# Seven products for one more block, and written-out lists of steps, in a linear attention and MLP kernel

## The chip, the core and the metric

The kernel runs on one core of a Trainium2 chip. A core has five engines that run side by side, each with a queue of its own that is worked off in order: TensorE (PE, matrix products, with its weight loads PEld), VectorE (DVE), ScalarE (ACT), GpSimd (POOL) and SyncE (SP). On POOL and SP stand mostly the issues of DMA transfers. Engines wait for each other by semaphores. The metric is the device time of one execution in microseconds (us), and the lower the better.

## The reference

Eight batches of 1024 tokens go through attention with 8 heads of 64, whose keys and values are first projected from 1024 positions to 64, and then through an MLP of 512 to 2048 to 512 without a gate.

```python
k_proj = einsum('ks,bhsd->bhkd', E, k)          # 64 x 64 per head
v_proj = einsum('ks,bhsd->bhkd', F, v)
attn = softmax(q @ k_proj.T / 8)                # 1024 x 64 per head
x = (attn @ v_proj) as [8192, 512]              # heads side by side
h = x @ w_in                                    # [8192, 2048]
out = (h * sigmoid(1.702 * h)) @ w_out          # [8192, 512]
```

Inputs and output are float32; the kernel multiplies in bfloat16 and adds up in float32.

## The kernel before

The 8192 tokens are cut into 16 blocks of 512 tokens, two blocks for a batch (block 2 and 3 belong to batch 1, block 4 and 5 to batch 2, and so on). All weights stay in SBUF. For a block the kernel computes scores and exponentials (`expT`), the sums of the exponentials, the values, and from them `xT` (the MLP's input, transposed, 512 rows by 512 tokens); then the first layer with its gelu into `gT`, and the second layer into `o0_sb` and `o1_sb`, which are stored. The work of neighbouring blocks is interleaved, so that the attention of later blocks runs beside the MLP of earlier ones.

**Products.** A plain first layer is `ffn1` (L420): 16 tiles of 4 matmuls of 128 x 128 weights on 512 columns, 64 in all. The other form splits both factors in two by two parts and forms the result with seven products of half size in place of eight (Strassen's scheme in Winograd's form). For the first layer these are the steps `u0` to `u3` (L657): four tiles, each with products P1 to P7 of 4 matmuls on 256 columns. They need sums of parts of `w_in` (`late`, 4 x 2048 elements in each partition, made once), sums of parts of the block's `xT` (`xw`, steps `xs.0` to `xs.3`), and per tile a chain on VectorE and ScalarE: c1 copies the accumulator A into a second bank B, c2 and c3 copy B and G to SBUF, d1 and d2 add, and g11, g12, g21, g22 are the gelus. For the second layer there are the products F1 to F7 (8 matmuls of 256 columns per half), the sums `gs1` to `gs4` of `gT`, the sums `tw` of `w_out`, and copies and additions Fc, Fo and Fd. Blocks 1 to 15 have the second layer in this form, blocks 3 to 15 the first layer.

**What sets the order.** Everything is written in the order in which it is issued; there is no scheduler, and each engine runs its own instructions in that order. Block 0 and 1, and block 2 up to its first layer, are loops over tiles, with further work put behind certain tiles by a table of slots (`at(j, slot, ...)`, L774): behind tile 15 and 16 of block 0, for example, the transposes of q (`q_tr`, L247) for block 1. In the first layer of block 2 stand `w_in_sums` (L477): six operations of VectorE on 2048 elements per partition, with `q_even`, a buffer of q, as temporary. From block 2's second layer on the order is a list of step names, `STEPS` (L586), gone through once for every j from 2 to 15: `u2.P5` is tile 2's product 5 of block j, `va.0+1` the values of block j+1, `F3.0-1` the second layer of block j-1. `AHEAD` (L872) inserts steps at the start, and `due` (L765) leaves out what the loops have done already. `BANK` (L597) gives each kind of tile one of the eight PSUM banks. In the last block the steps of the second layer are replaced by `ffn2_parts` (L517) with a list of its own.

**Other steps named below.** `sc` scores (16 matmuls in 2 halves, L698), `ex` exponentials on ScalarE, `gt` ScalarE's load of the gelu table, `su` and `den` sums of exponentials and their copy, `ga`, `rc`, `sr`, `sb` the gather of those sums into another layout, the reciprocal, the write to DRAM and the broadcast into `rbc`, `va` and `mv` the values and their product with `rbc`, `pj` the projection of k and v of a batch, `kb`, `vq` its copies out of PSUM and `kd` the transposing DMA of k, `qd` that of q, `ld` and `lq` the loads of k, v and q of the next batch on POOL's queue, `hold` a copy of one element on POOL that makes that queue wait for `kd`, `st` the stores. Blocks 1 and 2 take their values in the form `tok`, `x_tr` (L393, L408): values with tokens on the partitions, a reciprocal and product on VectorE, and transposes on PE.

Of the kernel before, what the change touches and what calls it, by code (L numbers as in the profile page):

```python
# [9 lines left out]
F32 = mybir.dt.float32  # L10
# [7 lines left out]
def kernel(ctx, tc, q, k, v, E, F,  # L18
# [53 lines left out]
    def load(b):  # L72
        for what in ("kvq", "kqv", "kvq", "qkv")[min(b, 4) - 1]:
            if what == "q":
                load_q(b)
            elif what == "k":
                load_kv(k, kt, b, "k_sb")
            else:
                load_kv(v, vt, b, "v_sb")
# [95 lines left out]
    kvps, qT, expT, xT, rbc, rdens = {}, {}, {}, {}, {}, {}  # L175
# [127 lines left out]
    def sums(h):  # L303


        def go():
            d_ps = [x_any([P, TB]), bank(5, [P, TB])]
            for p in range(HP):
                for e in range(2):
                    r = HI if (p + e) % 2 else LO  # L310
                    nc.tensor.matmul(d_ps[e][32 * p:32 * p + 32], ones[r, :32], expT[h][r, p, :], start=True, stop=True)
            den = att.tile([P, 2, TB], F32, name="den", bufs=1)
            for e in range(2):
                nc.vector.tensor_copy(den[:, e, :], d_ps[e])
            rdens[h] = den
        return go

    def gather(h):
        def go():
            n = 2 * HP * TB // P  # L320
            rc = att.tile([P, n], F32, name="rc")
            nc.sync.dma_start(out=rc, in_=rdens.pop(h)[0:P:32].rearrange("p e (r n) -> p (e r) n", n=n))
            rdens[h] = rc
        return go

    def spread(h, q=nc.sync, recip=True):
        def go():
            rc = rdens.pop(h)
            n = rc.shape[1]
            if recip:  # L330
                nc.vector.reciprocal(rc, rc)
            rdr = dram.tile([HP, 2, TB], F32, name="rdr")
            q.dma_start(out=rdr.rearrange("p e (r n) -> (p e r) n", n=n), in_=rc)
            rbc[h] = att.tile([P, HP, TB], F32, name="rbc", bufs=1)
            for e, r in enumerate((LO, HI)):
                q.dma_start(out=rbc[h][r], in_=rdr[None, :, e, :].to_broadcast([D, HP, TB]))
        return go

    def norm(h, u):
        def go():  # L340
            e = [expT[h][:, 2 * u + i, :] for i in range(2)]
            d_ps = [x_any([P, TB]) for _ in range(2)]
            eight(d_ps, [ones, ones], e)
            n_ps = [x_any([P, TB]) for _ in range(2)]
            eight(n_ps, [vqs[h // NB2 % 2][:, 2 * u + i, :] for i in range(2)], e)
            for i in range(2):
                rd = att.tile([P, TB], F32, name="rdn")
                nc.vector.reciprocal(rd, d_ps[i])
                nc.vector.tensor_tensor(x_of(h)[:, 2 * u + i, :], n_ps[i], rd, op=ALU.mult)
        return go  # L350

    def values(h, u):
        def go():
            n_ps = [x_any([P, TB]) for _ in range(2)]
            eight(n_ps, [vqs[h // NB2 % 2][:, 2 * u + i, :] for i in range(2)],
                  [expT[h][:, 2 * u + i, :] for i in range(2)])
            for i in range(2):
                nc.vector.tensor_tensor(x_of(h)[:, 2 * u + i, :], n_ps[i], rbc[h][:, 2 * u + i, :], op=ALU.mult)
        return go

# [114 lines left out]
    def w_in_sums():  # L477

        tmp = []

        def tt(out_, in0, in1, op=ALU.subtract):
            def go():
                if not tmp and None in (out_, in0, in1):
                    tmp.append(ldpool.tile([P, KC // 2, DH], F32, name="q_even"))
                a, b, c = (tmp[0] if x is None else x for x in (out_, in0, in1))
                nc.vector.tensor_tensor(a, b, c, op=op)
            return go

        return [tt(late[:, 0], a21, a22, ALU.add), tt(late[:, 2], a11, a21), tt(None, a21, a22, ALU.add),
                tt(None, None, a11), tt(late[:, 3], a12, None), lambda: nc.vector.tensor_copy(late[:, 1], tmp[0])]  # L490
# [26 lines left out]
    def ffn2_parts(j, d, e, f, last):  # L517

        b, c = divmod(j, NB2)
        ov = out[b * S:(b + 1) * S, :].rearrange("(p j) m -> p j m", j=J)[:, c * JB:(c + 1) * JB]
        o = [None, None]
        ops, of = ffn2_ops(j), OF
        gb, u = {}, {}
        split = last is not None

        def mm(i, tc_, first, final):
            a, w = ops[i]
            one = split and of[i] == 2  # L530
            for k in range(FH):
                dst = gb[2 + tc_][:, 0] if one else gb[of[i]][:, tc_]
                nc.tensor.matmul(dst, a[:, k, tc_ * P:(tc_ + 1) * P], w[:, k],  # L533
                                 start=(first and (one or tc_ == 0) and k == 0), stop=(final and k == FH - 1),
                                 skip_group_check=True)

        def tile_of(n, k):
            gb[n] = bank(k, [P, 2, MH])

        def put(t, n=0, m=2, ms=slice(0, DM)):  # L540
            nc.sync.dma_start(out=ov[:, 2 * t + n:2 * t + m, ms], in_=o[t][:, n:m, ms])

        def p(i, tc_):
            def go():
                if (i, tc_) == (1, 0):
                    tile_of(0, d)
                    for t in range(2):
                        o[t] = work.tile([P, 2, DM], F32, name=f"o{t}_sb", bufs=1)
                if (i, tc_) == (5, 0):
                    tile_of(2, f)  # L550
                    u[2] = work.tile([P, 2, MH], F32, name="u2_sb", bufs=1)
                if (i, tc_) == (5, 1) and split:
                    tile_of(3, last)
                mm(i, tc_, i in (1, 5), i in (2, 3, 4) and tc_ == 1)
                if split and i == 5:
                    nc.scalar.copy(u[2][:, tc_], gb[2 + tc_][:, 0])
                elif split and i == 3:
                    nc.vector.tensor_tensor(o[0][:, tc_, MH:], gb[2 + tc_][:, 0], u[1][:, tc_], op=ALU.add)
                    put(0, tc_, tc_ + 1, slice(MH, DM))
                elif tc_ == 0:  # L560
                    pass
                elif i == 1:
                    tile_of(1, e)
                    nc.scalar.copy(gb[1], gb[0])
                elif i == 5:
                    nc.scalar.copy(u[2], gb[2])
                elif i == 6:
                    u[1] = work.tile([P, 2, MH], F32, name="u1_sb", bufs=1)
                    nc.scalar.copy(u[1], gb[1])
                elif i == 2:  # L570
                    nc.scalar.copy(o[0][:, :, :MH], gb[0])
                    if split:
                        put(0, ms=slice(0, MH))
                elif i == 7:
                    nc.vector.tensor_tensor(o[1][:, :, MH:], gb[1], u[2], op=ALU.add)
                elif i == 4:
                    nc.scalar.copy(o[1][:, :, :MH], gb[1])
                    put(1)
                elif i == 3:
                    nc.vector.tensor_tensor(o[0][:, :, MH:], gb[2], u[1], op=ALU.add)  # L580
                    put(0)
            return go

        return {(i, t): p(i, t) for i in range(1, 8) for t in range(2)}

    STEPS = """  # L586
        F3.0-1 u2.c1 Fo1-1 u0.d2 rc+2 F3.1-1 u2.P5 u3.c3 u3.P7 u0.g22 Fd2-1 u2.P6 u0.g12 u2.c2 u2.c3 u2.P2
        u2.g11 u3.P3 va.0+1 u3.d1 st0-1 gs1.0 u3.P2 u3.d2 u3.g11 u2.P3 u3.g12 mv.0.1+1 u2.P7 va.1+1 pj+4 ld+4
        u3.g22 u3.P4 u2.d2 st1-1 u2.g12 u3.g21 u2.d1 mv.0.0+1 kb+4 F1.0 mv.1.0+1 u2.g22 vq.0+4 u2.P4 mv.1.1+1
        gs1.1 u2.g21 vq.1+4 F1.1 u0.P1+1 sr+2 sc.0+3 gs2.0 gs2.1 sc.1+3 Fc1 ex.0.0+3 gs3.0 u1.P1+1 xs.0+1  # L590
        ex.1.1+3 xs.2+1 gs3.1 F2.0 F2.1 ex.1.0+3 xs.1+1 kd+4 ex.0.1+3 F6.0 F6.1 Fc2 u0.c1+1 su+3 u1.c1+1 gt+1
        u0.P6+1 den.0+3 u0.P2+1 Fo0 den.1+3 gs4.1 u1.P6+1 F7.0 u1.P2+1 u1.P5+1 u0.c2+1 F5.0 u1.c2+1 u0.g11+1
        u1.c3+1 F5.1 ga+3 Fc3 u1.P7+1 F7.1 u1.g11+1 xs.3+1 gs4.0 u1.P3+1 u2.P1+1 u0.P5+1 u1.d1+1 u3.P1+1 Fd1
        u0.c3+1 u1.P4+1 F4.0 u0.P7+1 sb+2 u1.d2+1 u0.d1+1 qd+4 lq+4 u1.g21+1 u3.c1+1 F4.1 u1.g12+1 u3.P6+1
        u3.c2+1 u0.P4+1 u1.g22+1 u3.P5+1 u0.P3+1 u0.g21+1
    """.split()
    BANK = dict(FD=0, FB=4, FG=0, A0=6, A1=1, B0=7, B1=3, G0=2, G1=5, S10=5, S11=7, V00=4, V01=0,  # L597
                S00=3, S01=2, V10=6, V11=5, D0=2, D1=5, PJ=1)
    ON_ACT = ('Fc1', 'Fc3', 'c2.2', 'c3.0', 'c3.1', 'c3.2', 'c3.3', 'vq')

# [335 lines left out]
```

## Time and profile before

| what | value |
| --- | --- |
| median of 3 runs | 477.85 us (477.5 to 478.31) |
| profiled execution | 476.44 us |
| its span, first to last instruction | 474.7 us |
| busy PE, PEld, DVE, ACT, POOL | 463.9, 356.2, 316.6, 322.1, 83.2 us |
| DMA | 69.19 MB, mean 146 GB/s |
| granted TensorE clock | 1.00 of full speed throughout |
| a block in the steady part | 54.75 us for two (139.24 to 193.99) |

The profile is one execution, taken by the hardware profiler. Busy time is the time in which an engine had at least one instruction running; the ends of matmuls are modelled, so short gaps of PE can hide in it. Rows of a timeline give start, length, engine, line, operation, the tile written and the tile read, their shapes and count, and in brackets the idle time of the engine before it, with what ended it. The chain of work that ended last is followed back from the last instruction.

### The profile page before, as it was taken

The page shows a single profiled execution, that of the slowest core. Times are in us where ns is not written, and L with a number is a line of the kernel's source. Part 1 is how long each engine was busy: PE and PEld are TensorE (multiplying, and loading weights), DVE is VectorE, ACT ScalarE, POOL GpSimd, SP SyncE. Part 2 cuts the span into 40 slices and gives each one's busy share as a digit, 9 for nine tenths or more (in the row PEclk, how much of TensorE's full clock was granted, in tenths as well). Part 3 has the DMA queues.
Part 4 walks back from the last instruction along what each step waited for, and adds up shares of the span by engine and source line. Part 5 has one row for each costly group of instructions (what it writes and reads, how often), then busy time and mean ns, then how long its engine had stood idle before and what let it go on. Part 6 is the DMA issues. An engine that isn't in the chain of part 4 may idle for free.

```text
span 474.7 us, 10486 instructions
## 1 busy us (share of the span) xinstructions
PE 463.9 (98%) x4323; PEld 356.2 (75%) x4331; DVE 316.6 (67%) x587; ACT 322.1 (68%) x559; POOL 83.2 (18%) x104
## 2 busy tenths in 40 slices
PE   8999999998999999999999999999999999999997
PEld 4644447556778788887878788787888878888885
DVE  4503895498486776858686685868667685958562
ACT  2665456566696777868686786957687786758472
POOL 7562161061051200501050010500000000000000
PEclk9999999999999999999999999999999999999999
DMA  9999999989799999937999299942371403602022
GB/s 169 200 188 207 228 192 152 232 169 180 114 212 207 200 200 238 110 92 162 211 216 130 94 152 214 172 95 97 90 182 38 121 25 91 177 5 90 0 90 90
DMA packets 132964, 69.19 MB, mean 146 GB/s; under 512 B 98341, under 2 KB 122421, under 8 KB 132917
## 3 DMA queue, kind: packets, MB, share of 16 engines
q0 software_dynamic: 86816, 30.43, 57.5%
q1 hardware_dynamic: 46020, 37.84, 32.8%
q8 instruction: 34, 0.56, 0.5%
q10 hardware_dynamic: 80, 0.26, 0.2%
q14 instruction: 14, 0.11, 0.1%
HBM read 72.88 MB, written 16.99 MB: 189 GB/s over the span
## 4 chain that ended last, share of the span: by engine, by line
PE 91%; DMA 3%; ACT 3%; DVE 2%; POOL 1%; issue 1%; DVEq 0%; ACTq 0%; POOLq 0%
PE k_ps L677 34%; PE k_ps L637 33%; PE k_ps L426 9%; PE k_ps L533 5%; PE k_ps L273 3%; PE k_ps L438 3%; PE k_ps L183 3%; DMA v_sb<-in_v_dram 3%; ACT gT L693 1%; PE k_ps L719 1%; DVE xT L713 1%; POOL k_sb L58 0%; POOL v_sb L58 0%; PE k_ps L398 0%; PE k_ps L413 0%
## 5 line engine op out<-in xcount | busy, mean ns | idle before, releaser
L623 DVE TENSOR_TENSOR q_even<-k_ps,q_even 128x512 f32<-128x512 f32 x104 | 70.5, 689 | 54.4 <-PE k_ps L677 53.2
L677 PE MATMUL k_ps<-xw,late 128*128 128x256 bf16 x624 | 89.5, 273 | 0.6 <-DVE xw L499 0.6
L677 PEld LDWEIGHTS <-late 128*128 128x128 bf16 x832 | 80.4, 98 | 12.8 <-PE k_ps L637 2.3
L637 PEld LDWEIGHTS <-sg 128*128 128x128 bf16 x832 | 81.2, 98 | 10.7 <-issue 1.4
L693 ACT ACTIVATE gT<-k_ps 128x512 bf16<-128x512 f32 x104 | 62.3, 601 | 25.3 <-PE k_ps L677 23.7
L637 PE MATMUL k_ps<-tw,sg 128*128 128x256 bf16 x624 | 76.8, 273 | 0.3 <-DVE u_sb L620 0.3
L677 PEld LDWEIGHTS <-w_in_sb 128*128 128x128 bf16 x624 | 58.2, 98 | 18.1 <-issue 11.3
L637 PEld LDWEIGHTS <-gT 128*128 128x128 bf16 x624 | 61.0, 98 | 7.8 <-issue 0.4
L620 ACT COPY q_even<-k_ps 128x512 f32<-128x512 f32 x65 | 37.0, 591 | 42.8 <-PE k_ps L677 42.0
L677 PE MATMUL k_ps<-xT,w_in_sb 128*128 128x256 bf16 x416 | 62.2, 273 | 1.0 <-ACT vq L620 1.0
L693 ACT ACTIVATE gT<-q_even 128x512 bf16<-128x512 f32 x104 | 61.4, 631 | 0.0
L70 POOL DMA_DIRECT2D q_sb<-in_q_dram x48 | 42.1, 904 | 106.5 <-DMA qT<-q_sb 70.1
L637 PE MATMUL k_ps<-w_out_sb,gT 128*128 128x256 bf16 x416 | 51.6, 273 | 0.1
L426 PE MATMUL k_ps<-xT,w_in_sb 128*128 128x512 bf16 (+1 forms) x195 | 42.4, 370 | 0.3
L507 DVE TENSOR_TENSOR sg<-gT 128x1024 bf16<-128x1024 bf16 (+2 forms) x64 | 41.4, 649 | 1.6 <-ACT gT L693 1.5
L428 ACT ACTIVATE gT<-k_ps 128x512 bf16<-128x512 f32 (+1 forms) x50 | 28.9, 580 | 18.0 <-PE k_ps L426 17.7
L426 PEld LDWEIGHTS <-w_in_sb 128*128 128x128 bf16 x200 | 19.3, 98 | 21.3 <-issue 0.8
L713 DVE TENSOR_TENSOR xT<-k_ps,rbc 128x512 bf16<-128x512 f32 x52 | 33.5, 680 | 0.0
L677 PE MATMUL k_ps<-xw,w_in_sb 128*128 128x256 bf16 x208 | 31.3, 273 | 0.0
L677 PE MATMUL k_ps<-xT,late 128*128 128x256 bf16 x208 | 31.2, 273 | 0.0
L681 ACT COPY k_ps<-k_ps 128x512 f32<-128x512 f32 x52 | 29.2, 588 | 2.7 <-DVE xT L713 1.2
L620 DVE COPY q_even<-k_ps 128x512 f32<-128x512 f32 x39 | 25.7, 686 | 8.0 <-PE k_ps L677 8.0
(136 smaller groups left out, 561.2 us busy)
## 6 DMA issues: line engine op xcount, KB each, us to landing
out_dram<-o_sb SPq DMA_DIRECT2D x31, 512.0 KB
rbc<-rdr SPq DMA_DIRECT2D x24, 512.0 KB
k_sb<-in_k_dram POOLq DMA_DIRECT2D x7, 1024.0 KB, 10.2
v_sb<-in_v_dram POOLq DMA_DIRECT2D x7, 1024.0 KB, 15.2
q_sb<-in_q_dram POOLq DMA_DIRECT2D x48, 128.0 KB, 6.4
w_in_sb<-in_moe_w_in_dram POOLq DMA_DIRECT2D x8, 256.0 KB, 10.8
w_out_sb<-in_moe_w_out_dram POOLq DMA_DIRECT2D x4, 512.0 KB, 11.5
q_even<-in_q_dram POOLq DMA_DIRECT2D x12, 128.0 KB, 13.2
```

The costliest lines, as they stand in the source:

```text
L70: nc.gpsimd.dma_start(out=qt[b][:, j], in_=qv[:, j])
L426: nc.tensor.matmul(h_ps, w_in_sb[:, kc, fc * P:(fc + 1) * P], xT[j][:, kc, ts], start=(kc == 0), stop=(kc == KC - 1))
L428: nc.scalar.activation(gts[j][:, fc, ts], h_ps, AF.Gelu_apprx_sigmoid)
L507: nc.vector.tensor_tensor(t[i - 1], in0, in1, op=ALU.add if i == 1 else ALU.subtract)
L533: nc.tensor.matmul(dst, a[:, k, tc_ * P:(tc_ + 1) * P], w[:, k], start=(first and (one or tc_ == 0) and k == 0), stop=(final and k == FH - 1),
L620: (nc.scalar.copy if n in ON_ACT else nc.vector.tensor_copy)(out_, in_)
L623: nc.vector.tensor_tensor(out_, in0, in1, op=ALU.add)
L637: nc.tensor.matmul(live[n][:, t], x[:, c, t * P:(t + 1) * P], w[:, c], start=(i in (1, 5) and t == 0 and c == 0), stop=(i in (2, 3, 4) and ...
L677: nc.tensor.matmul(live[h][:, r], a[:, c, f:f + P], w[:, c], start=(i in (1, 5) and r == 0 and c == 0), stop=(i in (2, 3, 4) and r == 1 an ...
L681: nc.scalar.copy(new(f"B{m}", [P, 2, TH]), live[f"A{m}"])
L693: nc.scalar.activation(out_, in_, AF.Gelu_apprx_sigmoid)
L713: nc.vector.tensor_tensor(x_of(j)[:, u, :], live[f"V{p[1]}{t}"], rbc[j][:, u, :], op=ALU.mult)
```

## The change

1. The first layer of block 2 is made of the steps `u0` to `u3` instead of the 16 tiles of `ffn1`. For that the sums of `w_in` are made earlier: `w_in_sums(i)`, a quarter of the columns at a time, is put behind tiles 11, 13, 15 and 17 of block 0's first layer, with `rbc` as temporary. The temporaries of block 2's tiles 0 and 1 (c2, c3, d1, d2) lie in `rbc` too; those of tiles 2 and 3, and of all later blocks, in `q_even` as before.
2. What was loops and inserted steps from the end of block 1's first layer to the middle of block 4's is a written-out list, `OPEN`: every word is a step, its block, and its PSUM banks; `!` swaps a copy between VectorE and ScalarE. The values of block 2 (`tok`, `x_tr`) become the steps `tk`, `tm`, `xr`, `xc`. `STEPS` is gone through for j from 4 to 13 only, and the last two blocks are a second list, `END`. A tile is now kept under its block, so that tiles of one kind of two blocks can live at once in different banks.
3. The gather of block 3's sums goes from SP's queue to POOL's. In `STEPS` the loads of the next batch stand behind `kd` and `hold` in place of behind `pj`. A matmul on zeros after block 1's first layer (L864) goes away.

The arithmetic of the seven products, the loads and the stores are the same. The list `STEPS` differs in two places only: `ld+4` moves, `hold+4` comes in (`gt+1` becomes `gt`).

```diff
-    def w_in_sums():
-        tmp = []
+    def w_in_sums(i):
+        if not wtmp:
+            wtmp.append(att.tile([P, HP, TB], F32, name="rbc", bufs=1))
+        n = DFF // 8
+        f = slice(i * n, (i + 1) * n)
+        tmp = wtmp[0][:, i].rearrange("p (c f) -> p c f", c=KC // 2)
+        c11, c12, c21, c22 = (a[:, :, f] for a in (a11, a12, a21, a22))
...
+        tt(late[:, 0, :, f], c21, c22, ALU.add)
+        tt(late[:, 2, :, f], c11, c21)
+        tt(tmp, c21, c22, ALU.add)
+        tt(tmp, tmp, c11)
+        tt(late[:, 3, :, f], c12, tmp)
+        nc.vector.tensor_copy(late[:, 1, :, f], tmp)
...
-        u2.g11 u3.P3 va.0+1 u3.d1 st0-1 gs1.0 u3.P2 u3.d2 u3.g11 u2.P3 u3.g12 mv.0.1+1 u2.P7 va.1+1 pj+4 ld+4
...
+        xs.2+1 gs3.1 F2.0 F2.1 ex.1.0+3 xs.1+1 kd+4 hold+4 ld+4 ex.0.1+3 gt F6.0 F6.1 Fc2 u0.c1+1 su+3 u1.c1+1
...
+    OPEN = """
+        sc.0@2:0,1 F1.0@1:2 ex.0.1@2 ex.0.0@2 F1.1@1 Fc1@1!:3 sc.1@2:4,5 sc.0@3:6,7 ex.0.1@3 tk.1.1@2:1 ex.1.1@2
+        tk.0.0@2:0 ex.0.0@3 F6.0@1 sc.1@3:7,5 tm.1.1@2 tm.0.0@2 tk.1.0@2:1 xr.1.1@2:0 xc.1.1@2 tk.0.1@2:6
...
+        tm.2.1@2 F2.1@1 qd@4 xr.3.1@2:6 xc.1.0@2 xs.0@2 F7.0@1 tm.3.0@2 F5.1@1 xr.2.1@2:1 u1.P5@2:0 xc.3.1@2
+        tk.2.0@2:4 u0.P1@2:5 Fo0@1 u0.c1@2:2 u0.P5@2:6 xc.2.1@2 Fc3@1! u0.c3@2 F7.1@1 xs.1@2 tm.2.0@2 u0.P6@2
...
+        u0.d1@2 F4.0@1 F4.1@1 u1.P3@2 u1.c1@2:6 rc@3 u1.P6@2 pj@4:4 xs.3@2 u0.g12@2 u1.c2@2 u1.P7@2 u1.d2@2
+        Fo1@1 u1.P2@2 u3.P1@2:3 u1.d1@2 u0.g22@2 kb@4! u1.g12@2 u1.g22@2 u0.P4@2 kd@4 u1.P4@2 u2.P1@2:0 u0.P2@2
+        vq.0@4! gs1.0@2 F3.0@1 F3.1@1 u1.g21@2 u1.g11@2 u3.c1@2:6 u3.P2@2 u2.c1@2:1 vq.1@4! Fd2@1 u2.P6@2
...
+        u3.P3@2 ex.0.0@4 u2.P4@2 u2.d2@2 u3.d2@2 ex.0.1@4 sc.1@5:3,5 sb@3 ex.1.0@5 u3.d1@2 sc.0@5:7,2 su@4:4,0
+        u3.P4@2 den.0@4 ex.0.0@5 ex.1.1@5 va.0@3:3,7 den.1@4 F1.0@2:4 ex.0.1@5 gt@5 u2.g21@2 u3.g21@2 mv.0.0@3
...
+    END = """
...
+        u2.g22@15 F1.1@15 Fd2@14 u3.g12@15 u2.g12@15 gs1.1@15 Fc1@15:0 u1.P4@15 u3.P4@15 gs2.0@15 gs2.1@15
+        u0.g21@15 u1.g21@15 gs3.1@15 st0@14 F5.1@15:4 gs4.0@15 F6.0@15 F6.1@15 F5.0@15:3 Fc3.1@15 u2.P4@15
+        u3.g21@15 u2.g21@15 Fc2@15 F7.0@15 gs4.1@15 F7.1@15 F2.0@15 Fc3.0@15 Fd1@15 F2.1@15 F4.0@15 F4.1@15
+        Fo0@15 F3.0@15 Fd2.0@15 F3.1@15 Fd2.1@15 Fo1@15 sp.0@15 sp.1@15 sp.2@15 sp.3@15
...
-    def step(name, j, banks=None):
+    def step(name, j, banks=None, swap=False):
+        queue = nc.gpsimd if j == 3 else nc.sync
...
+                w = j == 2 and n < 2
+                if w not in uu:
+                    uu[w] = (att.tile([P, HP, TB], F32, name="rbc", bufs=1).rearrange("p i (r t) -> p i r t", r=2) if w
+                             else ldpool.tile([P, 4, 2, TH], F32, name="q_even"))
...
-    for i, f in enumerate(w_in_sums()):
-        at(2, (4, 6, 8, 10, 15, 15)[i], f)
+    for i in range(4):
+        at(0, 11 + 2 * i, lambda i=i: w_in_sums(i))
...
-            nc.tensor.matmul(bank(6, [P, TB]), zeros[:, :P], zeros, start=True, stop=True)
...
+    steps(OPEN)
+    for j in range(4, 14):
+        for word in STEPS:
...
+    steps(END)
```

## The prediction

> **What bounds the kernel now.** I read the page from the top: first the busy shares, then the slices, then the chain of work that ended last.
>
> ```profile
> PE 463.9 (98%) x4323; PEld 356.2 (75%) x4331; DVE 316.6 (67%) x587; ACT 322.1 (68%) x559; POOL 83.2 (18%) x104
> PE   8999999998999999999999999999999999999997
> ...
> PE 91%; DMA 3%; ACT 3%; DVE 2%; POOL 1%; issue 1%; DVEq 0%; ACTq 0%; POOLq 0%
> ```
>
> TensorE (PE) is the bound: 98% busy, 91% of the chain, and only the first, the tenth (107 to 119 us) and the last slice fall below 9. So a change pays only by matmul time that it removes or by gaps of PE that it closes. Next I asked for busy time by stretch, to see where the gaps are (columns: stretch, its length, then PE, weight loads, DVE, ACT, POOL with counts, clock, DMA share, GB/s).
>
> ```profile
> 69.00:86.00 17.00, 16.38 (x183) 12.94 (x181) 10.35 (x34) 10.13 (x16) 1.76 (x2) 1.00 1.75 164
> 102.00:124.00 22.00, 19.57 (x206) 13.39 (x205) 17.16 (x30) 12.53 (x22) 4.25 (x5) 1.00 1.36 149
> 139.20:167.50 28.30, 28.30 (x283) 22.89 (x281) 20.40 (x35) 20.88 (x38) 7.84 (x9) 1.00 1.67 193
> ```
>
> From 139 on a block runs without a gap, and the same list of steps runs there after the change, so nothing is to be had there. The gaps lie in the second layers of blocks 1 and 2 (69 to 86, 102 to 124), and at the end. The clock is 1.00 everywhere. Ends of matmuls are modelled, so I took the gaps from starts in PE's timeline:
>
> ```profile
> 70.72 0.63 PE L273 MATMUL k_ps<-qT,kt 64*32 64x512 bf16 x16
> 71.27 1.92 PE L533 MATMUL k_ps<-tw,sg 128*128 128x256 bf16 x16
> 73.40 0.40 PE L398 MATMUL k_ps<-vx,expT 128*128 128x130 bf16 x4 [0.21 <-ACT expT L292]
> ...
> 113.50 1.05 PE L637 MATMUL k_ps<-tw,sg 128*128 128x256 bf16 x8
> 115.14 0.61 PE L677 MATMUL k_ps<-xw,late 128*128 128x256 bf16 x4 [0.59 <-DVE xw L499]
> ...
> 123.99 0.60 PE L677 MATMUL k_ps<-xT,w_in_sb 128*128 128x256 bf16 x4 [1.04 <-ACT vq L620]
> ```
>
> Sixteen 256-column matmuls need 1.75 us (0.109 each; 32 take 3.49 in the chain), sixteen score matmuls 0.55 (70.72 to 71.27), eight 0.34. What a run of PE took beyond that is a gap: at 73.0 waiting for the exponential 0.38; the scores at 80.32 to 82.06 (they took 1.74) 1.19; 103.8 0.23; 106.5 0.47; 109.6 0.37; 111.4 0.42; 114.4 0.77 (VectorE's x sums); 122.8 1.22 (ScalarE's copies after the projection). Together **5.05 us**. The end of the chain:
>
> ```profile
> 454.71 1.08 ACT q_even L620 x2
> 455.79 4.03 ACT gT L693 x8
> 459.81 0.50 ACT k_ps L564
> 460.35 10.78 PE k_ps L533 x96
> ```
>
> ScalarE runs ten operations in a row and PE waits 0.86 us (459.49 to 460.35) for the copy at L564 before it goes on to the last 96 matmuls.
>
> **The change, part by part.** The sum is made against the profiled execution: span 474.7, its own time 476.44. The median of the runs shown is 477.85, 1.41 above it; I take the difference of times as the same for both.
>
> (1) Seven products in block 2's first layer. Out go 64 matmuls of 512 columns: 46 take 10.09 us in the chain, 0.219 each, so 14.04. In come 4 tiles of 7 products of 4 matmuls, 112 of 256 columns at 0.109: 12.21. The L864 matmul on zeros (0.22) goes too. Weight loads, 98 ns each, stay below 109 ns. **-2.05 us.** Around it VectorE gets 16 copies and additions (0.69 each, some given to ScalarE) and 4 x sums (0.42), and ScalarE 4 copies (0.59), while the w_in sums of 10.5 us (L486, L490: 2 x 1.19, 3 x 2.29, 1.22) leave VectorE there. Adding the durations of all steps of the list up to block 4 in their order gives PE 78.8 us, VectorE 63.1, ScalarE 61.6. PE stays the longest queue, so that work is hidden by matmuls; without that cover it would cost up to its own length.
>
> (2) The w_in sums in block 0. A call now does two bf16 operations (0.416, L499's row for 512 elements), three with float32 (0.689, L623's row) and a copy to bf16 (0.427, L155's row): 3.33 us, four calls 13.3. VectorE was nearly empty there, but its queue is in order, and PE's scores of block 1 wait for two copies in it:
>
> ```profile
> 34.52 0.69 DVE L256 COPY qT<-k_ps 128x1024 bf16<-128x1024 bf16 x1 [12.62 <-PE k_ps L254]
> ...
> 35.83 0.69 DVE L256 COPY qT<-k_ps 128x1024 bf16<-128x1024 bf16 x1 [0.62 <-PE k_ps L254]
> ...
> 38.31 0.63 PE L273 MATMUL k_ps<-qT,kt 64*32 64x512 bf16 x16
> ```
>
> Call 0 needs chunk 4 of w_in, which lands by 25.7 (POOL's issue at 25.74 waits for it, if each issue waits for the DMA eight places before it). It runs to 29.1, call 1 to 32.4. The first copy is at 34.52 as before, then call 2 from 35.2 to 38.5, and only then the second copy, to 39.25 instead of 36.5. The scores start at 39.3, not 38.31: **+1.0 us**. Call 3 ends at 42.6, before the next VectorE work that PE needs (41.78 now, 42.8 shifted). Ends: 0, if the float32 operations run at a quarter of the long rows (2.29/4 = 0.57), to +2.5, if the chunks land later and call 1 also sits before the first copy.
>
> POOL writes descriptors for w_out in this stretch, and a row shows what a VectorE copy from SBUF to SBUF does to that:
>
> ```profile
> 64.66 1.22 DVE L468 CAST tw<-rbc 128x2048 bf16<-128x2048 f32 x1
> ```
> ```profile
> 64.70 1.66 POOL L70 DMA_DIRECT2D q_even<-in_q_dram  x1
> ```
>
> The issue beside that copy took 1.66 us, against a median of 0.90; beside the 2.29 us addition before it (62.45) issues took 0.88. In the Trainium skill, "SBUF — State Buffer", sections "SBUF: two separate sides" and "Who interferes with whom", such copies can run in a mode that locks GpSimd out of a shared port, and a tensor_tensor does not block its writes; it advises to issue from another queue. By that rule the four new copies would push POOL back by at most 4 x 0.43 = 1.7 us (an estimate), and with it the first layer 2, were the transfer on the path; the gain below would be 1.7 us smaller. By the rows the first copy of a call ends at 29.1, after the first w_out issue at 25.74, whose data PE needs first (36.49; landed by 35.73), and the later chunks are needed several us after they land. I add 0.
>
> (3) Blocks 1 to 3 in an explicit order, a bank for each tile. This is where the 5.05 us of gaps are. The trace does not show the new order, so bounds: all gone (-5.05), or as many as before (0), or new ones (rival 3). I followed the first 18 us by the rows: after block 1's first layer ScalarE still needs 0.87 of gelu, 1.28 for the table and 0.61 for each exponential, and PE has 2.8 us of scores and F1 to cover it, leaving about 0.4; later u0.P6 waits for xs.1 behind five VectorE operations, about 0.5. The wait of 1.22 after the projection goes: its copies are now on VectorE (kb, vq), and PE has P4, P2, F3.0 and F3.1, over 3 us, beside them. I take 1.85 left of 5.05: **-3.2 us**, nearer to the full gain because VectorE and ScalarE each have 15 us to spare beside PE.
>
> The queues: the gather of block 3 goes from SP to POOL, behind the load of v for batch 2 (issued 74.47), before the spread and the loads of batch 3, and nothing on POOL is due before 92. In the steady blocks the loads now stand behind a POOL copy that waits for the transposed k: 164.06 plus some 3 us instead of 163; data are needed at the next projection, 216. Landing takes 10 to 23 us, so 0.
>
> (4) The end as a list. F5.1 and two P4 stand between F1.1 and F6.0, 1.75 us of matmuls, over ScalarE's two gelus and the copy (1.8 us). I take 0.6 of the 0.86: **-0.6 us** (ends -0.86 and +0.9, a gap of the same size elsewhere).
>
> Sum: -2.05 + 1.0 - 3.2 - 0.6 = -4.85. Profiled 476.44 to 471.6; median 477.85 to **473.0 us**.
>
> **Rivals.** (1) The lists move the gaps and close none: -2.05 + 1.0 = -1.05, 476.8. For it: PE's waits have six different releasers, and the pattern exponentials, table load, copies is still there. Against: 15 us of slack, and the longest gap (1.22) has one plain cause that the list removes. (2) All closes and the w_in sums hide: -2.05 - 5.05 - 0.86 = -7.96, 469.9. (3) Slower: the broadcast of block 3's reciprocals (sb@3, to rbc) comes too late. rbc now holds the temporaries of block 2's first two tiles, so POOL can issue it only after u1.g22, some 21.5 us into the list that begins at 69.7: 91 to 92.5. Before it was issued at 96.18 and the second half was in place at 103.98, where POOL waits for it: 7.8 us. So it lands near 100; VectorE needs it for mv.0.0 at 32.4 us into the list, 102.1. But the two stores of block 1 and the loads of batch 3 (3 MB) now share its stretch, and loads of 1 MB took up to 22.8 us to land. A landing after 107 eats the whole gain; at 111, 19 us after its issue, PE stands 9 us: 482, less what the list can put before it, some 480. Against: only 1 MB of that is queued before it.
>
> **How the numbers follow.** Forecast 0.60; rival 1 0.17, whose 476.8 lies at the border of what a measurement of this kernel can tell from no change (0.2%, 0.96 us), so 0.10 of it counts as faster and 0.07 as same; rival 2 0.13; rival 3 0.10. Faster 0.60 + 0.13 + 0.10 = 0.83, same 0.07, slower 0.10. The range goes from rival 2's 469.9 to 477.2, rival 1 with its uncertainty, and leaves rival 3 out.
>
> **What would show it.** Step 1: 112 more matmuls at L629 (256 columns, 0.109 apart), none of 512 columns after block 1. Step 2: the scores of block 1 start near 39.3, with qT's second copy ending just before; if they start at 38.3 that term is 0. Step 3: from 70 to 149 the sum of PE's gaps is near 2 us, and no wait is over 1; the start of block 4's run of 32 L575 matmuls, 167.5 now, comes near 163.3. Step 4: no wait of PE over 0.3 after 440. Wrong would be a wait of PE or VectorE for rbc or the loads of batch 3, or VectorE becoming the releaser of most of PE's waits up to 100.

## The result, and the profile after

The changed kernel takes **494.44 us** (median of 4 runs, 493.44 to 495.15) against 478.04 for the kernel before in the same session (477.5 to 478.31): ratio 1.0343 [1.032, 1.0366]. The forecast of 473.0 and its range up to 477.2 are missed, and on the other side: the change makes the kernel 3.4% slower. The profiled execution took 495.15 us, its span is 493.4.

The page of the changed kernel: busy shares, PE's slices, the clock's slices, and the chain of work that ended last.

```profile
PE 466.7 (95%) x4378; PEld 364.2 (74%) x4378; DVE 330.3 (67%) x623; ACT 321.4 (65%) x560; POOL 93.9 (19%) x109
...
PE   7999995999994999999999999999999999999997
...
PEclk9999997999997999999999999999999999999999
...
PE 68%; DMA 13%; ACT 9%; DVE 7%; issue 1%; POOL 1%; SPq 1%; ACTq 0%; DVEq 0%; POOLq 0%
```

PE is down from 98% to 95% of a longer span, and a DMA has come into the chain with 13%. PE's slices 7 and 13 (74 to 86 and 148 to 160 us) are half empty, and in the same two the clock falls, which was full throughout before. PE's waits in the changed kernel (what waited, for what, then us in total, times, longest):

```profile
PE k_ps L274 <- DMA qT<-q_sb: 11.6, 3, 6.2
PE k_ps L629 <- ACT k_ps L633: 5.8, 8, 0.9
PE k_ps L192 <- DMA k_sb<-in_k_dram: 1.8, 1, 1.8
```

The first two are new and large: the scores (L274) wait for the transposed q, which SP's DMA writes, and the products of the first layer (L629) for ScalarE's copy c1 (L633). The spans can be cut at the same three places: the end of block 1's first layer, and the starts of the runs of 32 second-layer matmuls of blocks 4 and 13. This shows where the time is lost (the last column is a kernel told below):

| stretch of the span | before | after | after minus before | e6_five |
| --- | --- | --- | --- | --- |
| start to end of block 1's first layer | 68.66 | 70.89 | +2.23 | 69.83 |
| to block 4's run (167.37, 180.53, 164.38) | 98.71 | 109.64 | +10.93 | 94.55 |
| to block 13's run (410.33, 430.41, 407.34) | 242.96 | 249.88 | +6.92 | 242.96 |
| to the end | 64.37 | 62.99 | -1.38 | 62.96 |

The 1.8 us for `k_sb` are not the change's: the same kernel profiled again (a2_again, below) has no wait over 0.3 us for its first loads, and its first row is +1.13 in place of +2.23. PE's timeline of the changed kernel at its two holes:

```profile
79.53 0.63 PE L274 MATMUL k_ps<-qT,kt 64*32 64x512 bf16 x8 [5.03 <-DMA qT<-q_sb]
...
154.24 1.06 PE L274 MATMUL k_ps<-qT,kt 64*32 64x512 bf16 x16 [6.23 <-DMA qT<-q_sb]
155.23 3.60 PE L575 MATMUL k_ps<-tw,sg 128*128 128x256 bf16 x16
```

The chain names what each hole waited for: a transposing DMA, from its issue to its landing.

```profile
65.32 14.17 DMA qT<-q_sb
...
132.81 21.29 DMA qT<-q_sb
```

The first is the second half of batch 1's q. Its scores, `sc.0@3`, stand eighth in `OPEN`; before, the table of slots asked for them at 80.32, and PE did not wait for q there, so the landing could not be seen. The second is q of batch 3 (`qd@6`). Here the surroundings have changed too. SP's queue, first of the kernel before and then of the changed one, and POOL's of the changed one:

```profile
124.64 8.90 SPq L263 DMA_TRANSPOSE qT<-q_sb  x1
```
```profile
127.52 1.20 SPq L722 DMA_TRANSPOSE kt<-k_b  x1
...
132.81 19.28 SPq L264 DMA_TRANSPOSE qT<-q_sb  x1
```
```profile
131.73 0.18 POOL L714 COPY held<-kt 1x1 bf16<-1x1 bf16 x1 [7.43 <-DMA kt<-k_b]
132.21 0.88 POOL L59 DMA_DIRECT2D k_sb<-in_k_dram  x1 [0.31 <-PE k_ps L629]
133.08 0.88 POOL L59 DMA_DIRECT2D v_sb<-in_v_dram  x1
```

Before, SP wrote q first and k after it (at 133.64), so `hold`, which waits for k, kept POOL's loads behind both. In `OPEN` k goes first; `hold@6` still waits for k alone, and lets 2 MB of loads go at 132.21, beside the transposes issued at 132.81. SP then needs 19.28 us for what took 8.90.

The 5.8 us in the second row of the waits come from ScalarE, in eight places. Its timeline before and after:

```profile
168.28 2.07 ACT L705 ACTIVATE expT<-k_ps 128x512 bf16<-128x512 f32 x4
170.21 1.12 ACT L681 COPY k_ps<-k_ps 128x512 f32<-128x512 f32 x2
171.34 1.28 ACT L296 ACT_TABLE_LOAD   x1
```
```profile
181.44 2.06 ACT L657 ACTIVATE expT<-k_ps 128x512 bf16<-128x512 f32 x4
183.52 1.28 ACT L297 ACT_TABLE_LOAD   x1
184.81 1.06 ACT L633 COPY k_ps<-k_ps 128x512 f32<-128x512 f32 x2
```

The table load now stands ahead of the two copies. The text of the change ahead of the prediction says that `STEPS` differs in two places; there is a **third**, which was overlooked: `gt` stood behind `u1.c1+1` and now stands ahead of `F6.0`.

### The profile page after: what moved, and what is told of

Read it like the earlier page. It is cut to its first block, busy times and chain, and to the rows that moved or that the text cites. A ratio compares the mean times of both kernels' runs of the same rounds, so it can differ in the third digit from the quotient of the medians.

```text
span 493.4 us, 10634 instructions
## 1 busy us (share of the span) xinstructions
PE 466.7 (95%) x4378; PEld 364.2 (74%) x4378; DVE 330.3 (67%) x623; ACT 321.4 (65%) x560; POOL 93.9 (19%) x109
## 4 chain that ended last, share of the span: by engine, by line
PE 68%; DMA 13%; ACT 9%; DVE 7%; issue 1%; POOL 1%; SPq 1%; ACTq 0%; DVEq 0%; POOLq 0%
PE k_ps L629 28%; PE k_ps L575 27%; DMA qT<-q_sb 11%; PE k_ps L367 4%; PE k_ps L184 3%; PE k_ps L379 2%; ACT expT L657 2%; DMA q_even<-in_q_dram 2%; PE k_ps L274 2%; ACT L297 2%; DVE sg L455 2%; ACT L657 1%; ACT gT L645 1%; DVE xT L665 1%; ACT k_ps L633 1%
## 5 line engine op out<-in xcount | busy, mean ns | idle before, releaser
L575 PEld LDWEIGHTS <-sg 128*128 128x128 bf16 x960 | 95.1, 99 | 13.5 <-issue 1.5
L629 PE MATMUL k_ps<-xw,late 128*128 128x256 bf16 x672 | 96.4, 273 | 5.9 <-ACT k_ps L633 5.8
L629 PEld LDWEIGHTS <-late 128*128 128x128 bf16 x896 | 87.4, 98 | 19.1 <-issue 6.9
L575 PE MATMUL k_ps<-tw,sg 128*128 128x256 bf16 x720 | 91.6, 279 | 0.0
L575 PEld LDWEIGHTS <-gT 128*128 128x128 bf16 x720 | 70.0, 98 | 9.1 <-issue 1.1
L629 PEld LDWEIGHTS <-w_in_sb 128*128 128x128 bf16 x672 | 63.4, 98 | 16.9 <-issue 9.7
L629 PE MATMUL k_ps<-xT,w_in_sb 128*128 128x256 bf16 x448 | 66.8, 273 | 0.1
L575 PE MATMUL k_ps<-w_out_sb,gT 128*128 128x256 bf16 x480 | 59.5, 273 | 0.0
L633 ACT COPY k_ps<-k_ps 128x512 f32<-128x512 f32 x56 | 31.2, 574 | 12.3 <-PE k_ps L629 10.2
L657 ACT ACTIVATE expT<-k_ps 128x512 bf16<-128x512 f32 x56 | 28.9, 606 | 13.5 <-PE k_ps L274 13.3
L560 DVE TENSOR_TENSOR o_sb<-k_ps,u_sb 128x512 f32<-128x512 f32 (+1 forms) x31 | 20.8, 673 | 21.8 <-PE k_ps L575 19.5
L629 PE MATMUL k_ps<-xw,w_in_sb 128*128 128x256 bf16 x224 | 33.4, 274 | 0.0
L629 PE MATMUL k_ps<-xT,late 128*128 128x256 bf16 x224 | 33.3, 273 | 0.0
L575 PE MATMUL k_ps<-tw,gT 128*128 128x256 bf16 x240 | 30.3, 273 | 0.0
```

The source lines that it names most:

```text
L560: nc.vector.tensor_tensor(out_, in0, in1, op=ALU.add)
L575: nc.tensor.matmul(at_(n)[:, 0 if one else t], x[:, c, t * P:(t + 1) * P], w[:, c], start=(i in (1, 5) and (one or t == 0) and c == 0), st ...
L629: nc.tensor.matmul(at_(h)[:, r], a[:, c, f:f + P], w[:, c], start=(i in (1, 5) and r == 0 and c == 0), stop=(i in (2, 3, 4) and r == 1 and ...
L633: nc.scalar.copy(new(f"B{m}", [P, 2, TH], f"B{n}"), at_(f"A{n}"))
L657: nc.scalar.activation(expT[j][:, 2 * u + t, :], at_(f"S{u}{t}"), AF.Exp, scale=scale)
```

## The experiments

The theory after reading the traces: the loss is (a) the table load ahead of the copies, (b) scores that ask too early for transposed q, (c) loads let go beside a transpose, and (d) the clock, which halves in both holes and so makes the work behind them slower. The rival: the list is at fault as a whole, and a wait taken away comes back at the next place.

**e1_gt_late**, (a) undone:

```diff
-        ex.0.1+3 gt F6.0 F6.1 Fc2 u0.c1+1 su+3 u1.c1+1 u0.P6+1
+        ex.0.1+3 F6.0 F6.1 Fc2 u0.c1+1 su+3 u1.c1+1 gt u0.P6+1
```

> The changed kernel with one step moved back: the load of the gelu table (gt) again stands behind the two copies u0.c1 and u1.c1 in the list of the steady blocks. Theory A (single steps in a wrong place): the ten waits of PE for the copy at L633, 0.7 to 0.9 us each, go; the time falls by 6 to 8 us, to about 487.5, and two steady blocks take 54.8 us again instead of 56.5. Rival B (the denser order makes some other wait take the place of each one removed): under 3 us fall, above 491.

489.06 us, 1.0245 [1.0227, 1.0263]: 5.4 less than after, where 6 to 8 were expected. All waits for L633 are gone, so (a) holds. Those for qT grew to 14.2 us in its profile: two of 1.53 and 1.22 now stand in the steady blocks, where the changed kernel had one of 0.37. From block 4's run to block 13's it takes 246.07 us, 3.81 less than after and 3.11 more than before. So a part of the gain is lost again at the next wait, as the rival has it.

**e2_fill**, (d) alone: PE is kept busy with products of zeros in both holes, 22 and 27 of 512 columns, which add work.

```diff
+                for _ in range(n):
+                    nc.tensor.matmul(w_ps, zeros[:, :P], zeros, start=True, stop=True)
...
+    FILL = {"sc.0@3:6,7": (6, 22), "sc.1@6:1,0": (1, 27)}
```

> The changed kernel with matmuls on zeros put in front of the two steps of the opening list that wait for a transposed q: 22 of 512 columns before the scores sc.0@3 (4.8 us), 27 before sc.1@6 (5.9 us). They compute nothing that is used. The waits stay, PE only has something to do in them. Theory A: the half clock that the trace shows from about 78 to 84.7 and from 153 to 158.5 us is there because PE stood still for 5 and 6 us; filled, the clock stays at 1.00 and the time falls by 4 to 5 us, to about 490. Rival C (the clock falls for another reason, such as the load on the DMA or the denser order): the clock falls again and the time stays within 1 us, or rises.

489.39 us, 1.0249 [1.0233, 1.0264]: 5.05 less than after, with 49 matmuls more. The clock of the changed kernel by stretch (stretch, length, PE, PEld, DVE, ACT, POOL, clock, DMA share, GB/s), and then that of e2_fill:

```profile
76.00:78.00 2.00, 0.00 (x0) 0.00 (x0) 0.00 (x0) 0.00 (x0) 0.87 (x1) 0.98 2.14 155
78.00:79.50 1.50, 0.00 (x0) 0.00 (x0) 0.00 (x0) 0.00 (x0) 0.00 (x0) 0.50 3.27 144
...
83.00:85.00 2.00, 2.00 (x15) 1.64 (x15) 1.32 (x5) 1.95 (x4) 0.00 (x0) 0.57 1.27 206
...
152.00:154.00 2.00, 0.00 (x0) 0.00 (x0) 0.00 (x0) 0.00 (x0) 0.00 (x0) 0.75 1.10 252
...
158.00:160.00 2.00, 2.00 (x12) 1.46 (x11) 1.14 (x2) 0.30 (x1) 2.00 (x4) 0.54 1.37 197
```
```profile
80.00:82.00 2.00, 2.00 (x28) 1.54 (x27) 1.55 (x6) 1.98 (x4) 0.00 (x0) 1.00 1.67 188
```

PE stood from 74.5 (79.53 less 5.03). What follows a hole runs at half clock: behind the second one, 16 matmuls of 256 columns at 155.23 take 3.60 us, elsewhere 1.91. The mean of 0.98 over 76 to 78 puts the fall at 77.9, and 0.57 over 83 to 85 the return at 84.7. So PE worked from 79.5 to 84.7 at half speed, which costs half of that, 2.6 us. The second hole gives 2.8 in the same way (154.24 to 159.8); together 5.4, and 5.05 were measured. In a2_again the clock came back sooner (81.7 and 156.8, PE back at 78.07 and 153.12): there the two stretches cost 3.7. In e2_fill the clock is 1.000 throughout, though PE still waited 0.51 and 0.46 us behind the zeros. (d) holds, at some 4 to 5 us.

**e3_hold_q**, (c) undone: `hold@6` reads an element of the transposed q, so the loads of batch 4 wait for it.

```diff
-            nc.gpsimd.tensor_copy(held, kts[b % 2][:1, 0, :1])
+            nc.gpsimd.tensor_copy(held, qT[b][:1, J - 1, HP - 1, P - 1:] if j == 6 else kts[b % 2][:1, 0, :1])
```

> The changed kernel with one operand changed: the one-element copy on POOL that stands before the loads of k and v of batch 4 (hold@6) reads the transposed q of batch 3 in place of the transposed k, so that these 2 MB are issued only when that q is in place. Theory A: q's transposes took 21.3 us to land (132.81 to 154.10) because the loads were issued beside them; alone they land in about 9 to 10 us, near 143, before the scores that need them at 147.9. The wait of 6.2 us and the half clock behind it (some 2.2 us) go: 8 to 9 us less, about 486. Rival D (transposes of 1024 tokens take some 20 us whatever runs beside them): the wait stays, time within 1 us.

484.0 us, 1.0136 [1.0121, 1.0151]: 10.4 less than after, the largest single part. SP's row and PE's first wait of e3_hold_q:

```profile
130.31 6.68 SPq L264 DMA_TRANSPOSE qT<-q_sb  x1
```
```profile
PE k_ps L274 <- DMA qT<-q_sb: 5.7, 2, 5.2
```

Without the loads of k and v beside it the same DMA takes 6.68 us in place of 19.28; the wait of 6.2 goes, and the 5.2 left are those of the first hole. (c) holds.

**e4_late_scores**, (b) undone: scores, exponentials and sums of block 3 stand later in `OPEN`, with other banks.

```diff
-        F1.1@1 Fc1@1!:3 sc.1@2:4,5 sc.0@3:6,7 ex.0.1@3 tk.1.1@2:1
+        F1.1@1 Fc1@1!:3 sc.1@2:4,5 tk.1.1@2:1
...
-        tm.2.1@2 F2.1@1 qd@4
+        tm.2.1@2 F2.1@1 sc.0@3:0,1 ex.0.1@3 ex.0.0@3 qd@4
...
-        F5.1@1 xr.2.1@2:1
+        F5.1@1 sc.1@3:4,5 ex.1.1@3 ex.1.0@3 gt@2 xr.2.1@2:1
```

> The changed kernel with the scores, exponentials and sums of block 3 (sc, ex, su, den, ga of block 3, and the gelu table load behind them) moved back in the opening list by some 5 us of matmuls, behind F2.1@1 and F5.1@1, in other banks; F7.1@1 moves up, rc@3 back. Theory A: the second half of q's transposes of batch 1 lands at 79.5 us whatever the order; the scores now ask for it at about 80, the wait of 5.0 us and the half clock behind it (some 2.7 us) go: 7 to 8 us less, about 487. Rival B: the work moved back makes a new wait of the same kind later (block 3's sums come too late for the broadcast), under 3 us less.

489.53 us, 1.0255 [1.0233, 1.0276]: 4.9 less than after, where 7 to 8 were expected. PE's waits of e4_late_scores:

```profile
PE k_ps L274 <- DMA qT<-q_sb: 7.6, 2, 7.2
PE k_ps L628 <- ACT k_ps L632: 6.7, 9, 1.2
```

The first hole is gone, but part of it came back: the moved steps brought new waits of 1.22 (for the copy u0.c1), 0.42 and 0.30 (at the sums of block 3). The second wait is 7.2, against 6.2 in the first profile of the changed kernel; as a2_again, with the order unchanged, has 7.33 there, this growth can't be put down to the edit. The rest of the shortfall was not traced. Here the rival is right in part.

**e5_three**: the edits of e1, e3 and e4 together.

> The changed kernel with all three repairs: the gelu table load behind the c1 copies, the loads of batch 4 held until the q of batch 3 is transposed, the scores of block 3 moved back. Theory A: the three are separate and add up, but for the late scores, whose gain of 4.9 us alone was cut because the next wait then grew to 7.2 us; that wait is gone here. From 494.4: 5.4, 10.4 and some 8 off, 470.5 to 472. Rival B (the gaps come back elsewhere): 476 or more, no better than the kernel before.

476.96 us (475.8 to 477.79), 0.9973 [0.9948, 0.9998]: 17.5 us less than after, but the 470.5 to 472 are missed. **a2_again**, the changed kernel once more beside it:

> The changed kernel once more, as a measure for its neighbours on the same chip. In the profile of it, the first load of k landed some 1.4 us later than in the profile before, and later kernels did not show that. If that belongs to the one profile: 493 to 494.5 us, and a start of block 0's first layer within 0.3 us of the kernel before. If it belongs to the kernel: the same late start again.

493.11 us, 1.0297 [1.0236, 1.0358], with waits of 13.1 for qT and 5.6 for L633 (11.6 and 5.8 in the first profile), and none over 0.3 for the first loads. This is 1.33 less than the 494.44 from which the gains above are counted. Against it e1 gains 4.1, e2 3.7, e3 9.1, e4 3.6 and e5_three 16.2, so each single gain is known to some 1.3 us only. With it e3 fits better: the second hole of a2_again, 7.33, and the half clock behind it, 1.84, make 9.2.

Two runs ask the same of the kernel before. **b1_gt_early** puts only its table load where the change has it, **b2_sums_early** only the sums of `w_in` into block 0.

```diff
-        ex.1.1+3 xs.2+1 gs3.1 F2.0 F2.1 ex.1.0+3 xs.1+1 kd+4 ex.0.1+3 F6.0 F6.1 Fc2 u0.c1+1 su+3 u1.c1+1 gt+1
+        ex.1.1+3 xs.2+1 gs3.1 F2.0 F2.1 ex.1.0+3 xs.1+1 kd+4 ex.0.1+3 gt+1 F6.0 F6.1 Fc2 u0.c1+1 su+3 u1.c1+1
```

> The kernel before with one step moved: the gelu table load (gt) in front of F6.0, ahead of the copies Fc2, u0.c1 and u1.c1 of its list, as in the changed kernel. Theory A: PE waits in nearly every block for the copy u0.c1, 0.7 to 0.9 us in eleven blocks, 6 to 8 us slower, 484 to 486. Rival B (it hurts only in the denser order of the changed kernel): within 1.5 us of 477.8.

485.38 us (median of four runs, one of them far off at 682.66), 1.0134 [1.0074, 1.0194], and in its profile 6.9 us of waits for the copy, ten of them, where there were none. So the place of one table load costs the kernel before 7.6 us by itself.

```diff
-    for i, f in enumerate(w_in_sums()):
-        at(2, (4, 6, 8, 10, 15, 15)[i], f)
+    for i in range(4):
+        at(0, 11 + 2 * i, lambda i=i: w_in_sums(i))
```

> The kernel before with the sums of w_in made in block 0 by quarters, as in the changed kernel, and block 2's first layer left as it is. Theory A: the second copy of q's transposes waits behind the third quarter, and PE's scores of block 1 start 0.6 to 1.0 us late; the 10.5 us of VectorE that leave block 2 were hidden, or shorten the gap at 114 by up to 0.8 us: 477.5 to 478.8. Rival E (the sums delay block 0 by more, as VectorE copies keep POOL from writing descriptors for w_out): 480 or more.

477.52 us, 0.9994 [0.9969, 1.0018]: no difference that can be told, though PE waits 0.5 us for the copy of qT, as after the change.

What still stood in e5_three? SP's transposes of q in its steady blocks, and PE waited 1.6 and 1.0 us for two of them:

```profile
174.21 15.53 SPq L264 DMA_TRANSPOSE qT<-q_sb  x1
```

The next, at 230.73, took 16.30; before they took 10.98 and 9.28. It is (c) again: `STEPS` lets the loads go 4 to 6 us later than before (POOL's k loads at 168.07 and 224.45, before 163.87 and 218.32), nearer to the transposes. **e7_loads_back** puts them back:

```diff
-        pj+4 u3.g22
+        pj+4 ld+4 u3.g22
...
-        kd+4 hold+4 ld+4 ex.0.1+3
+        kd+4 ex.0.1+3
```

> The kernel e5_three (476.96) with the loads of k and v in STEPS put back to where before had them: ld+4 behind pj+4, and hold+4 taken out. In e5_three SP needs 15.3 to 16.3 us for the transposes of q at 174, 231 and 287, against 9.3 to 11.0 before, and TensorE waits for two of them, 1.6 and 1.0 us. Theory (the loads now stand beside the transposes, so that they take longer): SP's rows fall to 9 to 11 us, both waits go, time 476.96 - 2.6 = 474.4. Rival (the loads beside them make no difference, or the time comes back in the next wait of the same blocks): SP's rows stay at 15 and the time stays within 1 us of 477.

473.66 us (473.13 to 475.51), 0.9926 [0.991, 0.9942]: 3.3 less than e5_three, with both waits gone. From block 4's run to block 13's it takes 242.96 us, as before the change, where e5_three takes 245.71. SP's row in e7_loads_back:

```profile
173.62 9.61 SPq L264 DMA_TRANSPOSE qT<-q_sb  x1
```

**e6_five** also moves two steps of `OPEN`, against the short waits that e4's edit brought:

```diff
-        sc.1@3:4,5 ex.1.1@3 ex.1.0@3 gt@2 xr.2.1@2:1
+        sc.1@3:4,5 ex.1.1@3 ex.1.0@3 xr.2.1@2:1
...
-        xr.2.0@2:4 u0.c2@2! xs.2@2
+        xr.2.0@2:4 u0.c2@2! gt@2 xs.2@2
...
-        u0.d1@2 su@3:6,4 den.1@3 den.0@3 ga@3 F4.0@1 F4.1@1
+        u0.d1@2 F4.0@1 su@3:6,4 den.1@3 den.0@3 ga@3 F4.1@1
```

> e7_loads_back, and two moves in the list of the opening: the load of the gelu table (gt@2) from behind the exponentials of block 3 to behind u0.c2@2, and F4.0@1 to ahead of the sums of block 3 (su@3). In e5_three TensorE waited 1.22 us for the copy u0.c1@2, behind the table load on ScalarE, and 0.72 for the two banks of su@3. Theory (what separates the repaired kernel from the forecast is these short waits): 474.4 - 1.2 - 0.7 = 472.5, next to the predicted 473.0. Rival (the lists move gaps and close none, so a wait that goes is back a few steps later): no gain over e7_loads_back, 474 or more, and over 476 if that too does nothing.

**472.68 us** (472.06 to 473.8), 0.9899 [0.9886, 0.9912]: 1.0% below the kernel before, and where the changed kernel was forecast. The two moves give 1.0 us of the 1.9 expected of them: the wait of 1.2 for the copy became two of 0.9 together. Its page and PE's largest remaining waits:

```profile
PE 461.7 (98%) x4372; PEld 360.9 (77%) x4378; DVE 330.4 (70%) x623; ACT 320.4 (68%) x560; POOL 84.2 (18%) x105
```
```profile
PE k_ps L152 <- DVE u_sb L117: 1.5, 1, 1.5
PE k_ps L628 <- ACT k_ps L632: 0.9, 2, 0.7
```

The rival, that the list is at fault as a whole, is ruled out: with a few steps put elsewhere, no wait over 0.7 is left but the 1.5 of the start, which every kernel here has, and PE's share is again 98%.

## Why the prediction was wrong

**"From 139 on ... the same list of steps runs there after the change, so nothing is to be had there."** This failed first, by a misreading of the diff. `gt` moved, ahead of two copies for which PE waits. Undone, this gives 3.81 of the +6.92 us in the third stretch of the table back (e1_gt_late, 4.1 to 5.4 us in all), and in the kernel before the move alone costs 7.6 (b1_gt_early). No view of the trace of before could have corrected this; comparing the two lists word by word would have, together with the ACT rows at 170.21 and 171.34.

**"The queues: ... Landing takes 10 to 23 us, so 0."** This was the largest loss. The step weighed the loads on POOL, whose data are needed late, and never asked what these loads do to SP's transposes of q beside them, nor when `OPEN` asks for the transposed q. Put back, the loads at `hold@6` give 9.1 to 10.4 us (e3_hold_q), those in the steady blocks 3.3 (from e5_three's 476.96 to e7_loads_back's 473.66), 2.75 of it in the third stretch.

**Step 3, "-3.2 us".** Its bounds ended at 0 and left the "new ones" to rival 3. I followed the first 18 us of the list by the rows of PE, VectorE and ScalarE, and gave a landing no duration: `sc.0@3` needed a DMA issued at 65.32 that landed at 79.5. Undone, that gives 3.6 to 4.9 (e4_late_scores).

**The clock** was no term at all. "The clock is 1.00 everywhere" was true of before, where PE's longest wait is 1.5 us; the two waits of 5 and 6 us, which the forecast missed, bring 3.7 to 5.05 more (e2_fill). These parts overlap, and their sum is more than the loss: a hole that closes takes its half-clock stretch along.

**What held.** The scores of block 1 were to start at 39.3 instead of 38.31; in e6_five they start at 39.21, after 0.54 us behind the copy of qT, and in the after profile at 40.38 with the same 0.54. The whole kernel lost nothing measurable by it (b2_sums_early). The 1.7 us that POOL could have lost beside VectorE's copies did not come: in a2_again two issues of w_out at 29.14, beside such a copy at 28.93, take 1.61 us, and 1.63 before. The end was to give 0.6 and gave 1.4 in both kernels of the table, the wait of 0.86 and some more. Rival 3 foresaw a landing that comes too late, but of another transfer: PE never waits for `rbc` to land, VectorE 0.5 us at most. In e6_five the first stretch is +1.17, the second -4.16 and the end -1.41, a sum of -4.40 for the forecast's -4.85 (+1.0, -2.05 - 3.2, -0.6). That this sum comes so near is partly luck: the second stretch gave 1.1 less than worked out and the end 0.8 more. It is also the sum of a repaired list; in the kernel that was forecast such gains lie hidden under the losses of four places. How the -4.16 divides between the seven products and the closed gaps was not tried; PE's busy time falls by 2.2 us (463.9 to 461.7) where 2.05 were worked out, though with modelled ends.

**What stays open.** Why the transpose at 65.32 takes 14 us was not tested: the loads of batch 2 run beside it in the kernel before too, where nobody waits for it and its landing can't be read.

## What to carry to other kernels

When an order is rewritten, compare the old and the new list word by word, and write down for every step that another engine waits for what now stands ahead of it on its own engine. A transfer that never shows as a wait has no known landing time: before a consumer is moved up, take the issue of its transfer plus the longest landing that any row shows for its kind, with what else is now in flight beside it. And a hole of PE of five us costs more than itself, because the work behind it starts at half clock.

## What the runs showed of the chip

- The clock fell to 0.50 some 3.4 us after PE stood still in the first hole (74.5 to 77.9) and 5.0 in the second (148.0 to 153.0), and came back 5.2 and 5.6 us after PE had begun again. In a2_again the same times are 2.1 and 4.2 us (72.8 to 74.9, 145.8 to 150.0) and 3.6 and 3.7. What stays the same in these four holes is the length of the half clock, 6.8 us each time (77.9 to 84.7, 153.0 to 159.8, 74.9 to 81.7, 150.0 to 156.8). In the Trainium skill, "TensorE: Matmul & The Clock Gate", section "Part 1: The HAM clock gate (the 'warmup' mystery)", the half clock is the default, and one window of about 3.4 us, idle or busy, switches it. The factor agrees with that, and 6.8 us are two such windows. But one fall came only 2.1 us after PE stood still, and every way back took longer than one window.
- Products of zeros count as work for the clock: with 49 of them in the two holes its mean is 1.000 where it was 0.986.
- The same transposing DMA of q (a batch, 1024 x 512 in bf16) kept SP for 6.68 us without the loads of k and v beside it (e3_hold_q) and for 19.28 with these 2 MB.
- ScalarE's load of the gelu table is 1.28 us in its row, and the copy behind it starts at once (183.52 + 1.28, then 184.81); the copies ran ahead of it and behind it alike, so they need not wait for a table.
